# Attention and two feed-forward layers on one core: the value products of a pair's first 256 queries in one visit of TensorE

## The chip, the cores and the metric

One core of a Trainium2 chip runs the whole program in one launch. The metric is the device time of one execution in microseconds (us); runs of one kernel differ by a few hundredths of a per cent here (1092.77 to 1093.15 us in three runs). Everything is fp32, and TensorE, VectorE (DVE), ScalarE (ACT), GpSimd (POOL) and SyncE (SP, which issues most DMAs) each work through a queue of their own in order.

## What is computed

Cut to what matters:

```python
# q, k, v: (4, 8, 576, 64)
q_rot, k_rot = rotate(q), rotate(k)                     # rotary embedding
scores = q_rot @ k_rot.T / 8
attn = exp(scores - max(scores))
attn = attn / (sum(attn) + 1e-9)
x = (attn @ v) as (2304 tokens, 512)
h = x @ w_in;   x = where(h > 0, h, exp(min(h, 0)) - 1) @ w_out       # first layer
h = x @ w2_in;  out = (h - tanh(h)) @ w2_out                          # second layer
```

The change is in the attention alone, in the line `attn @ v`.

## The kernel before

**Pairs and items.** The 32 heads are worked in 16 pairs (numbered 0 to 15). A pair has nine items: for each of the four blocks `u` of 128 queries one item per head (items 0 to 7), and item 8 holds the last 64 queries of both heads. The loop in the attention part runs over all 144 items; below, step s of a pair is the loop's turn `i = 9p + s`, so that steps 9 to 14 of a pair are also steps 0 to 5 of the next.

**One turn of the loop** emits, in this order:

- the row maximum of item i on DVE (`emit_max`, L241);
- the scores of item i + 1 on TensorE (`emit_s`, L232, into one of two PSUM buffers `s`). Each buffer is free again when the exponential two items earlier has read it;
- the exponential of item i on ACT (`emit_exp`, L255);
- `flush`: the copies out of PSUM that were put off in the turn before. Transposes go to `aT` and `aTr` (L286 on DVE, L288 on ACT), a finished product goes to `xa` (L293, always ACT). The transposes' copies are numbered through the whole run, and those whose number leaves 1 or 3 when divided by 5 go to DVE, the others to ACT;
- the normalisation of item i - 1 (`emit_norm`: L268, L269 on DVE, L272 on POOL);
- parts of the next pairs' rotation (`prep`: L148, L150, L153, L157) and of a weight's conversion (L74 to L92);
- the transposes of item i - 4 on TensorE (`emit_t`: L312, L322, and L316 for item 8), into one of three PSUM buffers `pt`;
- the value products that are due (`emit_pv`, L345).

**The value products.** A pair has three groups of queries: group 0 (items 0 to 3, 256 queries), group 1 (items 4 to 7) and group 2 (item 8). A group needs five chunks c of 128 keys, two matmuls each; on the engine each matmul is two weight loads and two matmul instructions, so that a chunk is 4 loads and a whole group is 20. The outputs are 64 wide (one head's dimension) and the moving side is 256 long. The groups 0 and 1 share the one PSUM buffer `o` in turn. The table `PV_AT` says, for each group and chunk, how many turns after the group's last transposes the chunk is emitted:

```python
PV_AT = ((1, 1, 1, 3, 3), (1, 1, 1, 3, 3), (2, 2, 2, 2, 2))
...
pend.append((i + PV_AT[uu // 2][c], pp, uu // 2, c))
```

The last transposes of group 0 are those of item 3, in step 7. So chunks 0 to 2 stand in step 8 and chunks 3 and 4 in step 10. The copy of item 3's transposes, which every chunk needs, is in the flush of step 8: on ACT it stands behind step 8's exponential, on DVE it stands behind step 8's maximum. By the numbering it is on DVE in pairs 2, 4, 7, 9, 12 and 14, and on ACT in the other ten.

**Step 8 to step 12 on TensorE**, before: scores 9, transposes of item 4, 12 loads of products | scores 10, transposes of item 5 | scores 11, transposes of item 6, 8 loads of products | scores 12, transposes of item 7 | scores 13, transposes of item 8 (whose last, L316, waits for the copy of item 7's transposes in the same step's flush), 12 loads of group 1. "Scores 10" are those of the item whose maximum is in step 10, that is of item 1 of the next pair.

**Keys and queries.** The rotated keys and queries of the next pair come through DMAs on SP's queue: `place` copies the second head's keys last (`k<-hl`, L194, four DMAs of a pair, issued after L157 in step 4). Scores 9 are the first that use the new pair's first head, scores 10 the first that use its second head. `load_v` (L137 to L141) loads a pair's values, and `load_w` (L64) a weight.

Of the kernel before, what the change touches and what calls it, by code (L numbers as in the profile page):

```python
# [23 lines left out]
def attention_elu_tanhshrink(ctx: ExitStack, tc: tile.TileContext, qk, v, w1i, w1o, w2i, w2o, tab, out):  # L24
# [35 lines left out]
    def load_w(key, eng=nc.sync):  # L60
        l, kind, c = key
        t = fm[:, 1024 * (nraw[0] % 2):1024 * (nraw[0] % 2) + 1024]
        nraw[0] += 1
        eng.dma_start(out=t.bitcast(mybir.dt.int64), in_=w_src[l, kind][c])  # L64
        raw_t[key] = t
# [43 lines left out]
    with ExitStack() as actx:  # L109
# [20 lines left out]
        def load_qk(p, x):  # L130
            t = p2.tile([128, 2, S], F32, tag=f"t{x}", name=f"t{x}")
            nc.sync.dma_start(out=t, in_=qk[p, :, 2 * x:2 * x + 2, :])
            t_t[p, x] = t

        def load_v(p):
            t = v_t[p] = vt_t[p % 2]
            nc.sync.dma_start(out=t[:, 0:512], in_=v[p, :, 0:512])  # L137
            for h in range(2):
                sl = slice(64 * h, 64 * h + 64)
                nc.sync.dma_start(out=t[sl, 512 + 64 * h:576 + 64 * h], in_=v[p, sl, 512:576])  # L140
            nc.sync.dma_start(out=t[64:128, 640:704], in_=v[p, 0:64, 512:576])  # L141
# [25 lines left out]
        def rotate_first(x):  # L167
            t = t_t.pop((0, x))
            prod = ps_s.tile([128, 2, 512], F32, tag="s", name="prod")[:, :, 0:288]
            for i in range(2):  # L170
                yield
                nc.vector.scalar_tensor_tensor(
                    out=two(t[:, 1, :]) if i else prod, in0=two(t[:, i, :]), scalar=(1.0 if x else SCALE),
                    in1=two(tabs[:, i, :]), op0=ALU.mult, op1=ALU.mult,
                )
            yield
            if x:
                nc.vector.tensor_tensor(out=two(rk), in0=prod, in1=two(t[:, 1, :]), op=ALU.add)
            else:
                for h in range(2):  # L180
                    sl = slice(64 * h, 64 * h + 64)
                    nc.vector.tensor_tensor(
                        out=two(rq[:, h, :])[sl], in0=prod[sl], in1=two(t[:, 1, :])[sl], op=ALU.add
                    )
            yield
# [53 lines left out]
        def emit_max(i):  # L239
            nm = sm.tile([128, 1], F32, tag="nm", name="nm")  # L240
            nc.vector.tensor_reduce(out=nm, in_=s_t[i][:, :, 0:288], axis=AX.XY, op=ALU.max, negate=True)  # L241
            nm_t[i] = nm

        def emit_exp(i):
            p, u, h = items[i]
            s = s_t.pop(i)
            if h in (0, None):
                if u < 4:
                    a_t[p, u] = p3.tile([128, 2, S], F32, tag="a", name="a")
                else:  # L250
                    a_t[p, u] = p1.tile([128, 1, S], F32, tag="a2", name="a2")
                n_t[p, u] = sm.tile([128, 2], F32, tag="den", name="den")
            a = a_t[p, u][:, h or 0, :]
            den = n_t[p, u][:, (h or 0):(h or 0) + 1]
            nc.scalar.activation(  # L255
                out=a.rearrange("p (x c) -> p x c", x=2), in_=s[:, :, 0:288], func=AF.Exp,
                bias=nm_t.pop(i), scale=1.0, accum_out=den,
            )

        def emit_norm(i):  # L260
            p, u, h = items[i]
            if h == 0:
                return
            nh = 2 if h == 1 else 1
            den = n_t.pop((p, u))[:, 0:nh]
            r = sm.tile([128, 2], F32, tag="r", name="r")
            for x in range(nh):
                nc.vector.tensor_scalar_add(den[:, x:x + 1], den[:, x:x + 1], 1e-9)  # L268
            nc.vector.reciprocal(out=r[:, 0:nh], in_=den)  # L269
            for x in range(nh):  # L270
                a = a_t[p, u][:, x, :]
                nc.gpsimd.tensor_scalar(  # L272
                    out=a, in0=a, scalar1=r[:, x:x + 1], scalar2=1.0, op0=ALU.mult, op1=ALU.mult
                )
# [7 lines left out]
        def flush():  # L282
            for out_, in_ in late:
                ev[0] += 1
                if ev[0] % 5 in (1, 3):
                    nc.vector.tensor_copy(out_, in_)  # L286
                else:
                    nc.scalar.copy(out_, in_)  # L288
            late.clear()
            for p, grp, o, n in late_x:  # L290
                b, hp = divmod(p, 4)
                x0 = NTOK * hp + b * S + 256 * grp
                nc.scalar.copy(out=xa[:, x0:x0 + n], in_=o[:, 0:n])  # L293
            late_x.clear()
# [75 lines left out]
        with tc.manual_schedule():  # L370
            for x in range(2):
                t_t[0, x] = p2.tile([128, 2, S], F32, tag=f"t{x}", name=f"t{x}")
            for i in range(2):
                nc.sync.dma_start(out=t_t[0, 1][:, i, :], in_=qk[0, :, 2 + i, :])
                nc.sync.dma_start(out=tabs[:, i, :], in_=tab[:, i, :])
                nc.sync.dma_start(out=t_t[0, 0][:, i, :], in_=qk[0, :, i, :])
            load_qk(1, 1)
            load_qk(1, 0)
            nc.vector.memset(xa[:, 0:512], 0.0)
            nc.vector.memset(zero, 0.0)  # L380
            nc.gpsimd.memset(rq[64:128, 0, :], 0.0)
            nc.gpsimd.memset(rq[0:64, 1, :], 0.0)
            make_identity(nc, ident)
            warm = ps_t.tile([128, 512], F32, tag="pt", name="warm")
            for i in range(8):
                nc.tensor.matmul(out=warm, lhsT=xa[:, 0:128], rhs=xa[:, 0:512], start=True, stop=True)
            for i in range(2):
                nc.scalar.copy(out=qa_t[i][:, S:640], in_=zero)
                nc.scalar.copy(out=qb_t[i][:, 0:64], in_=zero)
                nc.gpsimd.memset(vt_t[i][64:128, 512:576], 0.0)  # L390
                nc.gpsimd.memset(vt_t[i][0:64, 576:704], 0.0)
            rot = [rotate_first(1), rotate_first(0)]
            for i in range(4):
                for r in rot:
                    next(r)
            n = len(items)
            pend = []
            nw = list(range(len(first_w)))[::-1]
            emit_s(0)
            load_v(0)  # L400
            PV_AT = ((1, 1, 1, 3, 3), (1, 1, 1, 3, 3), (2, 2, 2, 2, 2))
            for i in range(n + D + 1):
                p, r = divmod(i, NI)
                for f, *arg in sched.get(i, ()):
                    if f is not prep:
                        f(*arg)
                if i == 7 or i % (2 * NI) == 12:
                    load_w(first_w[nw.pop()]) if nw else None
                if i < n:
                    emit_max(i)  # L410
                if i + 1 < n:
                    emit_s(i + 1)
                if i < n:
                    emit_exp(i)
                flush()
                if 0 <= i - 1 < n:
                    emit_norm(i - 1)
                if p < NPAIR:
                    for f, *arg in sched.get(i, ()):
                        if f is prep:  # L420
                            f(*arg)
                    c = r if p == 1 else NI * (p % 2) + r - 3 if p else -1
                    if c >= 0 and c % 2 == 0 and c // 2 < NCV and p // 2 < len(first_w):
                        key = first_w[p // 2]
                        conv_w(key, c // 2, 512 * (p // 2 % 3))
                if 0 <= i - D < n:
                    emit_t(i - D)
                    pp, uu, hh = items[i - D]
                    if uu in (1, 3) and hh == 1 or uu == 4:
                        for c in range(5):  # L430
                            pend.append((i + PV_AT[uu // 2][c], pp, uu // 2, c))
                for x in [x for x in pend if x[0] <= i]:
                    emit_pv(*x[1:])
                    pend.remove(x)
                if n - 8 <= i < n and (i - n) % 2 == 0:
                    split_x(0, (i - n + 8) // 2)
            while pend:
                emit_pv(*pend.pop(0)[1:])
            flush()
# [521 lines left out]
```

## Time and profile before

| | before |
|---|---|
| median of 3 runs | 1093.11 us (1092.77 to 1093.15) |
| the profiled execution: its own time / its span | 1093.27 us / 1090.8 us |
| TensorE matmul (PE) busy | 1066.9 us, 98% of the span, 6480 instructions |
| TensorE weight loads (PEld) busy | 959.0 us, 88% |
| VectorE busy | 753.3 us, 69% |
| ScalarE busy | 723.1 us, 66% |
| GpSimd busy | 696.5 us, 64% |
| granted TensorE clock | 1.00 of full speed |
| stretch with value products (L345) | 27.4 to 302.7 us |

Matmuls are pipelined and their ends are modelled, so a busy PE need not be PE at its peak. In the attention the weight loads (PEld) show better when TensorE moves on: every matmul has a load of its own, and a load that starts late tells of a wait. The first number of a timeline's row is the start in us from the start of the span, the second how long it lasted; what stands in brackets is idle time of the engine before it, and what ended it.

### The profile page before, as it was taken

The page shows a single profiled execution, that of the slowest core. Times are in us where ns is not written, and L with a number is a line of the kernel's source. Part 1 is how long each engine was busy: PE and PEld are TensorE (multiplying, and loading weights), DVE is VectorE, ACT ScalarE, POOL GpSimd, SP SyncE. Part 2 cuts the span into 40 slices and gives each one's busy share as a digit, 9 for nine tenths or more (in the row PEclk, how much of TensorE's full clock was granted, in tenths as well). Part 3 has the DMA queues.
Part 4 walks back from the last instruction along what each step waited for, and adds up shares of the span by engine and source line. Part 5 has one row for each costly group of instructions (what it writes and reads, how often), then busy time and mean ns, then how long its engine had stood idle before and what let it go on. Part 6 is the DMA issues. An engine that isn't in the chain of part 4 may idle for free.

```text
span 1090.8 us, 18762 instructions
## 1 busy us (share of the span) xinstructions
PE 1066.9 (98%) x6480; PEld 959.0 (88%) x6480; DVE 753.3 (69%) x1436; ACT 723.1 (66%) x1560; POOL 696.5 (64%) x653
## 2 busy tenths in 40 slices
PE   8999999999999999999999999999999999999998
PEld 4777777777799999999999999988998999889986
DVE  7898888888546456675675665376766667766674
ACT  3677677777668656555555555588777877878762
POOL 5887888887568755555555556566567555755552
PEclk9999999999999999999999999999999999999999
DMA  7878777776224344354344672265545664556531
GB/s 237 224 185 214 178 206 195 206 199 173 59 69 143 129 153 136 117 164 166 115 145 139 216 260 81 94 224 202 175 163 176 248 212 175 176 167 221 172 126 58
DMA packets 86590, 182.75 MB, mean 168 GB/s; under 512 B 11745, under 2 KB 47585, under 8 KB 86497
## 3 DMA queue, kind: packets, MB, share of 16 engines
q1 hardware_dynamic: 78720, 153.25, 44.7%
q10 hardware_dynamic: 7776, 28.32, 8.7%
q8 instruction: 51, 0.84, 0.3%
q14 instruction: 43, 0.34, 0.1%
HBM read 127.21 MB, written 27.79 MB: 142 GB/s over the span
## 4 chain that ended last, share of the span: by engine, by line
PE 76%; DVE 11%; POOL 4%; ACT 3%; DMA 3%; issue 2%; SPq 0%; ACTq 0%; DVEq 0%; POOLq 0%
PE y L529 18%; PE h L472 18%; PE yb L723 14%; PE hb L758 9%; PE o L345 6%; PE s L232 5%; PE cvb L758 3%; PE pt L312 3%; DVE nm L241 3%; DVE aT L286 1%; DVE fn L791 1%; DMA qb<-hl 1%; ACT a L255 1%; POOL blk L513 1%; DVE t L150 1%
## 5 line engine op out<-in xcount | busy, mean ns | idle before, releaser
L513 POOL TENSOR_TENSOR gt<-fn,gt 128x384 fp32r<-128x384 f32 x119 | 123.1, 1035 | 78.2 <-ACT gt L512 66.2
L272 POOL TENSOR_SCALAR a<-a,r 128x576 f32<-128x576 f32 x144 | 138.4, 973 | 48.2 <-DVE r L269 31.1
L255 ACT ACTIVATE a<-s,nm 128x576 f32<-128x576 f32 x144 | 107.0, 743 | 90.7 <-DVE nm L241 76.0
L723 PE MATMUL yb<-wb,blk 128*128 128x512 f32 x603 | 154.3, 392 | 0.4 <-POOL blk L513 0.4
L758 PE MATMUL hb<-blk,wa 128*128 128x384 f32 x720 | 139.9, 337 | 2.0 <-DVE fn L791 2.0
L758 PEld LDWEIGHTS hb<-blk,wa 128*128 128x128 f32 x720 | 127.1, 188 | 7.3 <-DVE fn L791 3.0
L723 PEld LDWEIGHTS yb<-wb,blk 128*128 128x128 f32 x603 | 112.5, 188 | 22.6 <-POOL blk L513 0.8
L480 ACT ACTIVATE fn<-h 128x384 f32<-128x384 f32 x96 | 47.3, 493 | 128.4 <-PE h L472 109.6
L241 DVE TENSOR_REDUCE nm<-s 128x1 f32<-128x576 f32 x144 | 107.9, 752 | 28.3 <-PE s L232 25.1
L513 POOL TENSOR_TENSOR blk<-fn,blk 128x384 fp32r<-128x384 f32 x67 | 71.1, 1061 | 87.9 <-ACT blk L512 59.6
L472 PE MATMUL h<-blk,wa 128*128 128x384 f32 x576 | 107.8, 335 | 0.8 <-POOL blk L55 0.6
L529 PE MATMUL y<-gt,wa 128*128 128x384 f32 x576 | 107.7, 334 | 0.1
L529 PE MATMUL y<-gt,wb 128*128 128x384 f32 x576 | 107.5, 334 | 0.0
L472 PE MATMUL h<-blk,wb 128*128 128x384 f32 x576 | 107.5, 334 | 0.0
L497 DVE TENSOR_SCALAR cvb<-fm 128x512 f32<-128x512 f32 x56 | 38.9, 694 | 98.1 <-ACT fm L495 95.7
L472 PEld LDWEIGHTS h<-blk,wa 128*128 128x128 f32 x576 | 100.3, 188 | 1.8 <-POOL blk L55 0.9
L529 PEld LDWEIGHTS y<-gt,wa 128*128 128x128 f32 x576 | 100.5, 188 | 0.4 <-issue 0.4
L529 PEld LDWEIGHTS y<-gt,wb 128*128 128x128 f32 x576 | 100.5, 188 | 0.0
L472 PEld LDWEIGHTS h<-blk,wb 128*128 128x128 f32 x576 | 100.5, 188 | 0.0
L92 POOL TENSOR_TENSOR fm<-fm,fn 128x512 fp32r<-128x512 f32 (+1 forms) x48 | 58.3, 1218 | 55.8 <-ACT fn L91 52.5
L345 PE MATMUL o<-aT,v 128*64 128x256 f32 (+1 forms) x768 | 89.5, 336 | 3.2 <-ACT aT L288 2.8
L148 POOL TENSOR_TENSOR t<-t,tabs 128x576 f32<-128x576 f32 x58 | 82.9, 1430 | 7.2 <-DMA t<-in_qk 7.2
(136 smaller groups left out, 2290.3 us busy)
## 6 DMA issues: line engine op xcount, KB each, us to landing
wa<-wi SPq DMA_DIRECT2D x96, 448.0 KB, 4.9
wb<-wo SPq DMA_DIRECT2D x48, 512.0 KB, 6.4
t<-in_qk SPq DMA_DIRECT2D x30, 576.0 KB, 5.1
k<-hl SPq DMA_DIRECT2D x60, 288.0 KB, 4.4
fm<-in_w2o ACTq DMA_DIRECT2D x16, 512.0 KB, 3.6
fm<-in_w2i ACTq DMA_DIRECT2D x14, 512.0 KB, 3.7
fm<-in_w1i ACTq DMA_DIRECT2D x12, 512.0 KB, 3.7
wi<-fn SPq DMA_DIRECT2D x24, 256.0 KB, 2.2
```

Of the source, the lines that this page charges most:

```text
L92: nc.gpsimd.tensor_tensor(out=lo, in0=f, in1=hi.bitcast(F32), op=ALU.subtract)
L148: eng.tensor_tensor(out=t[:, i, :], in0=t[:, i, :], in1=tabs[:, i, :], op=ALU.mult)
L232: nc.tensor.matmul(out=s[:, half, o0:o0 + n], lhsT=w, rhs=k[:, part, c0:c0 + n], start=(m == 0 and part == 0), stop=(m == len(terms) - 1 a ...
L241: nc.vector.tensor_reduce(out=nm, in_=s_t[i][:, :, 0:288], axis=AX.XY, op=ALU.max, negate=True)
L255: nc.scalar.activation(out=a.rearrange("p (x c) -> p x c", x=2), in_=s[:, :, 0:288], func=AF.Exp, bias=nm_t.pop(i), scale=1.0, accum_out=den,)
L272: nc.gpsimd.tensor_scalar(out=a, in0=a, scalar1=r[:, x:x + 1], scalar2=1.0, op0=ALU.mult, op1=ALU.mult)
L345: nc.tensor.matmul(out=o[sl, 0:n], lhsT=w, rhs=m, start=(c == 0), stop=(c == 4))
L472: nc.tensor.matmul(out=hp, lhsT=w[:, wp, ws], rhs=x_hl(t, xp, c), start=(m == 0), stop=(m == 3 * KC - 1))
L513: nc.gpsimd.tensor_tensor(out=g[:, 1, :], in0=f, in1=g[:, 0, :].bitcast(F32), op=ALU.subtract)
L529: nc.tensor.matmul(out=y_t[e][:, 0:NB], lhsT=w[:, wp, es], rhs=gt[:, gp, :], start=st, stop=sp)
L723: nc.tensor.matmul(out=y, lhsT=gt[:, gp, es], rhs=w[:, wp, :], start=(j == 0 and k == 0), stop=(j == NJ - 1 and k == 2))
L758: nc.tensor.matmul(out=bank, lhsT=w[:, wp, o:o + 128], rhs=x[:, xp, cc, :], start=(start and k == 0), stop=(stop and k == 5), skip_group_c ...
```

## The change

One row of the table: all five chunks of group 0 two turns behind its last transposes, that is in step 9, rather than three chunks in step 8 and two in step 10. Groups 1 and 2 stay.

```diff
-            PV_AT = ((1, 1, 1, 3, 3), (1, 1, 1, 3, 3), (2, 2, 2, 2, 2))
+            PV_AT = ((2, 2, 2, 2, 2), (1, 1, 1, 3, 3), (2, 2, 2, 2, 2))
```

On TensorE's queue, at steps 8 to 10 of pair 0 (`s` scores, `pt` and `pr` transposes, `o` value products of two heads, each row of `o` with x6 standing for 12 loads):

```order
 L232 MATMUL s<-k_193,qa_93 128x288 x4
 L312 MATMUL pt<-ident,a 128x128 x4
-L345 MATMUL o<-aT,v_96 64x256 x6
 L232 MATMUL s<-k_196,qb_95 128x288 x4
 L312 MATMUL pt<-ident,a 128x128 x4
 L322 MATMUL pr<-ident,a 128x128
+L345 MATMUL o<-aT,v_96 64x256 x8
+L345 MATMUL o<-aTr,v_96 64x256 x2
 L232 MATMUL s<-k_193,qa_93 128x288 x4
 L312 MATMUL pt<-ident,a 128x128 x4
-L345 MATMUL o<-aT,v_96 64x256 x2
-L345 MATMUL o<-aTr,v_96 64x256 x2
```

Scores 10 (the fourth row) now stand directly behind step 8's transposes, and all twenty loads of the group stand between step 9's transposes and scores 11 (the row behind them). Scores 12, after the last row, have no products directly before them any more.

On ACT's queue the copy of the finished group 0 (`xa`, the L293 row with 256 columns) is flushed one turn earlier. At the same place of the program (`a` exponentials, `aT` and `aTr` copies of transposes):

```order
 L255 ACTIVATE a,den<-s,nm 128x576
 L288 COPY aTr<-pr 128x128
-L255 ACTIVATE a,den<-s,nm 128x576
-L288 COPY aT<-pt 128x4x128
-L293 COPY xa<-o 128x256
+L293 COPY xa<-o 128x256
+L255 ACTIVATE a,den<-s,nm 128x576
+L288 COPY aT<-pt 128x4x128
 L255 ACTIVATE a,den<-s,nm 128x576
 L288 COPY aTr<-pr 128x128
```

The copy now stands between the exponentials of steps 10 and 11. On SP's queue one load of a weight of the second layer stands earlier, ahead of the last-but-one pair's key copies (`fm` is the buffer of raw weights):

```order
 L64 DMA fm<-in_w1o 128x512
+L64 DMA fm<-in_w2i 128x512
 L194 DMA k_3570<-hl_3532 64x1152 x2
 L194 DMA k_3573<-hl_3532 64x1152 x2
```

The instructions of DVE and POOL stand in the order that they had.

## Rows read from the trace of the kernel before

**Rows 1.** Waits of PEld from 16 to 303 us: total us, times, longest.

```profile
PEld s L232 <- issue: 11.2, 29, 0.4
PEld o L345 <- ACT aT L288: 9.9, 15, 1.5
```

**Rows 2.** Timeline of PEld, pair 8: start us, us, what, and idle before it.

```profile
173.00 1.05 PEld L345 LDWEIGHTS o<-aT,v 128*64 128x64 f32 x10 [0.77 <-ACT aT L288]
174.44 0.56 PEld L232 LDWEIGHTS s<-k,qb 128*128 128x128 f32 x4 [0.38 <-issue]
...
175.40 0.14 PEld L322 LDWEIGHTS pr<-ident,a 128*128 128x128 f32 x1
...
176.02 0.49 PEld L312 LDWEIGHTS pt<-ident,a 128*128 128x128 f32 x4
...
177.69 0.56 PEld L232 LDWEIGHTS s<-k,qb 128*128 128x128 f32 x4 [0.39 <-ACT aT L288]
```

**Rows 3.** Timeline of ACT, pair 8, step 8.

```profile
171.64 0.74 ACT L255 ACTIVATE a<-s,nm 128x576 f32<-128x576 f32 x1 [0.40 <-DVE nm L241]
...
172.37 0.57 ACT L288 COPY aT<-pt 128x512 f32<-128x512 f32 x1
```

**Rows 4.** Timeline of DVE, pair 8, steps 11 and 12.

```profile
176.35 0.76 DVE L241 TENSOR_REDUCE nm<-s 128x1 f32<-128x576 f32 x1
...
178.53 0.76 DVE L241 TENSOR_REDUCE nm<-s 128x1 f32<-128x576 f32 x1 [0.43 <-PE s L232]
```

**Rows 5.** Timeline of PEld, pair 7.

```profile
153.99 0.49 PEld L312 LDWEIGHTS pt<-ident,a 128*128 128x128 f32 x4
154.64 1.06 PEld L345 LDWEIGHTS o<-aT,v 128*64 128x64 f32 x12 [0.17 <-issue]
156.09 0.56 PEld L232 LDWEIGHTS s<-k,qb 128*128 128x128 f32 x4 [0.39 <-issue]
...
162.61 0.14 PEld L316 LDWEIGHTS pr<-ident,a 128*128 128x128 f32 x1 [1.04 <-ACT aT L288]
```

**Rows 6.** Timeline of ACT, pair 7, step 8.

```profile
154.16 0.74 ACT L255 ACTIVATE a<-s,nm 128x576 f32<-128x576 f32 x1
```

**Rows 7.** Timeline of DVE, pair 7, steps 8, 11 and 12.

```profile
153.86 0.68 DVE L286 COPY aT<-pt 128x512 f32<-128x512 f32 x1
...
158.21 0.75 DVE L241 TENSOR_REDUCE nm<-s 128x1 f32<-128x576 f32 x1
...
160.46 0.75 DVE L241 TENSOR_REDUCE nm<-s 128x1 f32<-128x576 f32 x1
```

**Rows 8.** Line L194: fourth key copy in pairs 2, 8, 14; issue, time to landing.

```profile
L194 SPq DMA_DIRECT2D k<-hl x1: 1433/1433/1433, 59.2 to 59.2; - x1
...
DMA to landing us min/median/max: 6.5/6.5/6.5
...
L194 SPq DMA_DIRECT2D k<-hl x1: 1442/1442/1442, 166.6 to 166.6; - x1
...
DMA to landing us min/median/max: 7.0/7.0/7.0
...
L194 SPq DMA_DIRECT2D k<-hl x1: 1145/1145/1145, 271.7 to 271.7; - x1
...
DMA to landing us min/median/max: 6.2/6.2/6.2
```

**Rows 9.** Timeline of DVE, pair 2 step 11, pair 14 steps 11 and 12.

```profile
68.70 0.74 DVE L241 TENSOR_REDUCE nm<-s 128x1 f32<-128x576 f32 x1
...
280.31 0.76 DVE L241 TENSOR_REDUCE nm<-s 128x1 f32<-128x576 f32 x1 [0.29 <-PE s L232]
...
282.49 0.76 DVE L241 TENSOR_REDUCE nm<-s 128x1 f32<-128x576 f32 x1 [0.50 <-PE s L232]
```

**Rows 10.** Timeline of SP's queue, 246 to 254 us.

```profile
246.61 0.55 SPq L64 DMA_DIRECT2D fm<-in_w1o  x1
252.94 1.11 SPq L194 DMA_DIRECT2D k<-hl  x2
```

## The prediction

> **What bounds the kernel now.** The page's busy shares come first: the matmul row is 98% busy, but its ends are modelled, so the waits of the weight loads decide. In the attention stretch two of them belong to the value products [rows 1]: 11.2 us in 29 idle gaps of up to 0.4 us ahead of scores, which nothing that the profile shows ended, and 9.9 us in 15 gaps ahead of products, ended by an ACT copy of transposes. The gaps ahead of scores stand behind product visits, and the second kind is what the change can remove. Next come the timelines, one pair of each sort.
>
> Pair 8 has the copy of item 3's transposes on ACT. Step 8's exponential ends at 171.64 + 0.74 = 172.38, the copy behind it at 172.37 + 0.57 = 172.94 [rows 3], and TensorE's product visit, two loads in, resumes at 173.00 [rows 2]: a stall of 0.77 us. Scores 10 follow at 174.44.
>
> Pair 7 has that copy on DVE. It ends at 153.86 + 0.68 = 154.54 [rows 7], 0.4 us before step 8's exponential does, 154.16 + 0.74 = 154.90 [rows 6]. The visit starts at 154.64, runs its 12 loads without a stall, and scores 10 stand at 156.09 [rows 5].
>
> What ends a pair's middle part is in step 12. The last transposes (L316) need the copy of item 7's transposes, which stands behind step 12's maximum: in pair 7 they wait 1.04 us for it, until 162.61 [rows 5]. Step 12's maximum in turn follows step 11's at once on DVE, or waits for scores 12. So the chain of interest is: scores 11, maximum 11, DVE's work of step 11, maximum 12, copy, L316. TensorE alone does not decide it. Behind L316 the rest of the pair hangs on TensorE's queue, so I let a delay of maximum 12 stay in the end time.
>
> **The change, term by term.** No instruction is added or dropped. Scores 10 lose the 12 loads in front of them, scores 11 get 20 loads in front of them, scores 12 lose 8.
>
> *When can scores 10 start?* Their PSUM buffer is the one that step 8's exponential reads. So they cannot start before that exponential ends, plus the 0.06 us by which loads follow what releases them (172.94 to 173.00 [rows 2, 3]). Before, products filled this time; now TensorE idles. This is the wait that the change adds, and everything behind it on TensorE's queue waits too.
>
> *From scores 10 to maximum 11.* Scores 10 and the transposes of step 9 take 1.10 us (174.44 to 175.40 + 0.14 [rows 2]). A visit of 12 loads takes from the end of the transposes to the next scores 153.99 + 0.49 = 154.48 to 156.09 = 1.61 us [rows 5]; one of 8 loads 176.02 + 0.49 = 176.51 to 177.69 = 1.18 us [rows 2]. That is 0.43 us for four, hence 1.61 + 2 x 0.43 = 2.47 us for 20. From the start of scores to the start of their maximum, where DVE waits for them, are 0.84 us (177.69 to 178.53 [rows 2, 4]). Sum: 4.41 us. So maximum 11 cannot start before the release of scores 10 + 0.06 + 4.41.
>
> *The six pairs with the copy on DVE.* Pair 7: 154.90 + 4.47 = 159.37 against 158.21 [rows 6, 7], 1.16 us later. DVE is busy from there to maximum 12 (158.21 to 160.46, 2.25 us), so the delay reaches it whole. There was no stall to gain from: only the two visits become one, and the larger one stands on the chain.
>
> *The ten with the copy on ACT.* Here the stall pays for most of it. Pair 8 by its exponential: 172.38 + 4.47 = 176.85 against 176.35. DVE's work of step 11 takes 178.53 - 0.43 - 176.35 = 1.75 us [rows 4], which puts maximum 12 at 178.60 against 178.53: before, it waited 0.43 us for scores 12, now it waits for maximum 11, and the two come out alike, 0 to 0.1 us.
>
> *The keys.* Scores 10 are the first that use the second head's new keys, and these were hidden: the fourth copy of pair 8 lands at 166.6 + 7.0 = 173.6 [rows 8], 0.84 us before scores 10 start now, but 1.2 us after the exponential that would release them. With 173.6 as the release, maximum 11 is at 178.07 and maximum 12 at 179.82 against 178.53: 1.29 us. In pair 2 it lands at 59.2 + 6.5 = 65.7, maximum 11 at 70.17 against 68.70 [rows 9]: 1.47 us. In pair 14 it lands at 271.7 + 6.2 = 277.9, maximum 11 at 282.37; DVE's step 11 takes 282.49 - 0.50 - 280.31 = 1.68 us [rows 9], maximum 12 is at 284.05 against 282.49: 1.56 us.
>
> *All pairs by the same working.* The six with the copy on DVE (first pair 2, last pair 14): 1.5, 1.1, 1.2, 1.6, 0.7, 1.6, together 7.7 us. Eight with it on ACT (pairs 1, 3, 5, 6, 8, 10, 11, 13): 0.2, 0.4, 0.2, 0.1, 1.3, 0.1, 0.7, 0.7, together 3.6 us. In pair 0 a long wait for the first DMAs follows, which hides either sign: 0. In pair 15 no scores follow, so one visit fewer gains: 1.61 + 1.18 - 2.47 = 0.32 us. Without the late keys the same sums give 6.0 and 0.5 us.
>
> *Moved on other queues.* ACT's copy of the finished group waits for the 20 loads with step 11's exponential behind it; but that exponential needs maximum 11, which ends over a microsecond after those loads, so nothing is paid. SP's weight load that is moved up costs one issue of 0.55 us in a queue that stands idle from 247.2 to 252.94 [rows 10]: nothing, unless its transfer delays key copies; bound 0 to one issue.
>
> *Sum.* The profiled execution took 1093.27 us with a span of 1090.8; the other 2.5 us lie around the span and stay. 1093.3 + 7.7 + 3.6 - 0.3 = 1104.3 us; the median of the runs is 0.2 us lower, so I say **1104.0 us**. Bounds: the release could cost 0.14 rather than 0.06 us, over 14 pairs + 1.1 us; key copies that land 0.5 us earlier or later relative to the rest take back or add some 3 us.
>
> **Row against rule.** The gaps ahead of scores [rows 1] and 0.17 us ahead of products [rows 5] are paid per visit, and the 0.32 us by which one visit is shorter than two is what they leave. The Trainium skill (TensorEngine Tiling (Array Packing), Key Properties) has a reason for such gaps: a change of the tiling mode, here between 128 x 128 and 128 x 64, drains TensorE; the trace agrees that there is a gap on each side of a visit. By that rule alone the change is a gain, the first rival below.
>
> **Rivals.**
> - *Faster: TensorE is the limit, and the saved visit counts.* Sixteen pairs by 0.32 us give 5.1 us: 1088.2 us. The 98% speak for it, and so does the stall of pair 8. Against it: maximum 12 and L316 are reached through DVE in pair 7, where TensorE waits 1.04 us [rows 5] whatever it did before. It decides if maximum 11 is not what maximum 12 waits for, that is if DVE has more than the 1.2 us of slack that I see none of in pair 7.
> - *The keys stay hidden.* If the key copies land earlier than now, with less traffic at their side, 6.0 + 0.5 - 0.3 remain: 1093.3 + 6.2 - 0.2 = 1099.3 us. For it: usual landings would do, and the late ones are collisions that may move.
> - *Taken back.* The delay of L316 could be slack before the next pair's step 8, where DVE or POOL would have waited anyway: about 1093 us. Against it: TensorE's queue runs from L316 to the next pair's step 8 with hardly a gap.
>
> **Chances.** The forecast with late keys 0.55, hidden keys 0.24, above the range 0.04, taken back 0.07, faster 0.10. A measurement of this kernel can tell about 0.2%, 2.2 us, from no change. So slower has 0.83, same 0.07, faster 0.10. The range 1097.5 to 1106.5 holds the forecast with its bounds and the hidden keys, 0.79 of the chance, and leaves out no change and faster.
>
> **What would show it.** In the changed profile: no stall within a product visit of 20 loads in step 9; scores 10 starting 0.06 us behind step 8's exponential, or behind a key copy's landing, with idle time of TensorE before them; maximum 11 some 4.4 us later; in pairs 2, 4, 7, 9, 12 and 14 L316 later by about a microsecond against the pair's step 8, in the others hardly unless keys are late. The time from the attention's end to the end of the program should stay as it is. I am wrong if scores 11 come no later than before relative to step 8, or if the pairs lengthen without these waits.

## The result and the profile after

The changed kernel takes 1106.49 us (median of four runs, 1105.73 to 1108.06), beside 1093.13 us for the kernel before: a ratio of 1.0124, 95% interval 1.0106 to 1.0141. The prediction said slower, and why; its 1104.0 us was 2.5 us too low, and its range ended at 1106.5.

| | before | after |
|---|---|---|
| the profiled execution: its own time / its span | 1093.27 / 1090.8 us | 1106.37 / 1103.5 us |
| TensorE matmul (PE) busy | 1066.9 us, 98% | 1064.7 us, 96% |
| VectorE / ScalarE / GpSimd busy | 753.3 / 723.1 / 696.5 us | 751.9 / 724.9 / 695.9 us |
| mean granted TensorE clock | 1.000 | 0.998 |
| start of the last value product | 302.7 us | 315.5 us |

No engine has more instructions, and busy times move by 2.2 us at most; what has grown is waits. The waits of TensorE's weight loads in the attention of the changed kernel (total us, times, longest):

```profile
PEld s L232 <- ACT a L255: 22.0, 40, 1.2
PEld s L232 <- issue: 7.3, 18, 0.8
...
PEld pr L316 <- ACT aT L288: 5.0, 3, 1.7
...
PEld o L345 <- ACT aT L288: 3.9, 6, 0.7
```

The stalls in front of products fell from 9.9 us to 3.9, and the gaps ahead of scores that nothing ended from 11.2 to 7.3 [rows 1], the latter in part by name alone: the 0.38 us behind pair 7's visit (below) now stand under an ACT copy. In their place scores wait for exponentials for 22.0 us, against 4.5 us before. DVE's maxima in turn wait more for scores. The page's row for them (busy, mean ns, idle before and what ended most of it), of the kernel before:

```profile
L241 DVE TENSOR_REDUCE nm<-s 128x1 f32<-128x576 f32 x144 | 107.9, 752 | 28.3 <-PE s L232 25.1
```

and of the changed one, with 15.4 us more idle time ended by scores:

```profile
L241 DVE TENSOR_REDUCE nm<-s 128x1 f32<-128x576 f32 x144 | 107.6, 750 | 42.1 <-PE s L232 40.5
```

**Pair 7**, with the copy of item 3's transposes on DVE. Timeline of PEld, changed kernel (answers to [rows 5]):

```profile
158.44 0.56 PEld L232 LDWEIGHTS s<-k,qb 128*128 128x128 f32 x4 [0.91 <-ACT aTr L288]
...
159.72 1.49 PEld L345 LDWEIGHTS o<-aT,v 128*64 128x64 f32 x16 [0.17 <-issue]
161.28 0.36 PEld L345 LDWEIGHTS o<-aTr,v 128*64 128x64 f32 x4
162.03 0.56 PEld L232 LDWEIGHTS s<-k,qa 128*128 128x128 f32 x4 [0.38 <-ACT aTr L288]
...
167.27 0.14 PEld L316 LDWEIGHTS pr<-ident,a 128*128 128x128 f32 x1 [1.68 <-ACT aT L288]
```

ACT's timeline in the same pair, step 8 (answers to [rows 6]):

```profile
157.43 0.74 ACT L255 ACTIVATE a<-s,nm 128x576 f32<-128x576 f32 x1
```

and DVE's, maximum 11 and behind it one row with the maxima 12 and 13 (answers to [rows 7]):

```profile
162.86 0.76 DVE L241 TENSOR_REDUCE nm<-s 128x1 f32<-128x576 f32 x1 [1.96 <-PE s L232]
...
165.13 1.42 DVE L241 TENSOR_REDUCE nm<-s 128x1 f32<-128x576 f32 x2
```

Step 8's exponential ends at 158.17, scores 10 start at 158.44, the 20 loads run without a stall, and from scores 10 to maximum 11 (162.86) are 4.42 us; the prediction had 4.41. Maximum 11 comes 4.69 us behind the exponential's end, against 3.31 before (154.90 to 158.21 [rows 6, 7]). Maximum 12 comes 6.96 us behind it, against 5.56 [rows 7]: the whole 1.4 us arrive there, DVE had no slack. L316 waits 1.68 us instead of 1.04.

**Pair 8**, the copy on ACT. Scores 10 in PEld's timeline of the changed kernel (answers to [rows 2]):

```profile
178.26 0.57 PEld L232 LDWEIGHTS s<-k,qb 128*128 128x128 f32 x4 [1.72 <-ACT aT L288]
```

Step 8's exponential in ACT's timeline (answers to [rows 3]):

```profile
176.31 0.74 ACT L255 ACTIVATE a<-s,nm 128x576 f32<-128x576 f32 x1 [0.43 <-DVE nm L241]
```

Maxima 11 and 12 in DVE's timeline (answers to [rows 4]):

```profile
182.69 0.76 DVE L241 TENSOR_REDUCE nm<-s 128x1 f32<-128x576 f32 x1 [2.35 <-PE s L232]
...
184.36 0.75 DVE L241 TENSOR_REDUCE nm<-s 128x1 f32<-128x576 f32 x1
```

The fourth key copy, by its line: issue and time to landing (answers to [rows 8]):

```profile
L194 SPq DMA_DIRECT2D k<-hl x1: 1443/1443/1443, 171.2 to 171.2; - x1
...
DMA to landing us min/median/max: 6.9/6.9/6.9
```

The exponential ends at 177.05, but the keys land at 171.2 + 6.9 = 178.1: scores 10 start 1.21 us behind the exponential, after 1.72 us of TensorE's idle time. The row puts that down to a copy on ACT, but the copy behind this exponential was done 0.6 us before, and the key is what came last. Maximum 12 is at 184.36 - 177.05 = 7.31 us behind the exponential, against 178.53 - 172.38 = 6.15 [rows 3, 4]: 1.16 us, where 1.29 were worked out.

**What was not predicted** is behind L316 in pair 12. PEld's timeline of the changed kernel there:

```profile
258.62 0.49 PEld L312 LDWEIGHTS pt<-ident,a 128*128 128x128 f32 x4
260.78 0.14 PEld L316 LDWEIGHTS pr<-ident,a 128*128 128x128 f32 x1 [1.67 <-ACT aT L288]
261.04 0.30 PEld L345 LDWEIGHTS o<-aT,v 128*64 128x64 f32 x4
261.53 0.23 PEld L345 LDWEIGHTS o<-aT,v 128*64 128x64 f32 x2 [0.19 <-issue]
...
263.80 0.82 PEld L232 LDWEIGHTS s<-k,qb 128*128 128x128 f32 x4 [0.76 <-issue]
```

and of the kernel before at the same place:

```profile
250.42 0.14 PEld L316 LDWEIGHTS pr<-ident,a 128*128 128x128 f32 x1 [1.57 <-ACT aT L288]
250.68 1.06 PEld L345 LDWEIGHTS o<-aT,v 128*64 128x64 f32 x12
252.13 0.56 PEld L232 LDWEIGHTS s<-k,qb 128*128 128x128 f32 x4 [0.39 <-issue]
```

The 12 loads and the gap behind them take 263.80 - 261.04 = 2.76 us instead of 252.13 - 250.68 = 1.45. The view by windows of the changed kernel says why (start and end of the window, its length, then PE, PEld, DVE, ACT and POOL busy with their instructions, the granted clock, DMA share, GB/s):

```profile
252.00:260.00 8.00, 7.08 (x54) 5.47 (x54) 7.16 (x16) 4.55 (x12) 6.12 (x6) 1.00 0.96 298
260.00:265.00 5.00, 4.22 (x20) 2.57 (x21) 2.79 (x7) 2.36 (x8) 5.00 (x6) 0.66 0.35 115
```

TensorE's clock fell to 1.2 GHz (0.5) from 260.97 to 264.38 us, right behind its wait of 1.67 us for L316. The kernel before waits 1.57 us at that place and keeps 2.4 GHz.

### The profile page after: what moved, and what is told of

Its sections match the earlier page's. It is cut to its first block, busy times and chain, and to the rows that moved or that the text cites. A ratio compares the mean times of both kernels' runs of the same rounds, so it can differ in the third digit from the quotient of the medians.

```text
span 1103.5 us, 18762 instructions
## 1 busy us (share of the span) xinstructions
PE 1064.7 (96%) x6480; PEld 958.9 (87%) x6480; DVE 751.9 (68%) x1436; ACT 724.9 (66%) x1560; POOL 695.9 (63%) x653
## 4 chain that ended last, share of the span: by engine, by line
PE 74%; DVE 11%; POOL 5%; ACT 4%; DMA 3%; issue 3%; SPq 0%; ACTq 0%; POOLq 0%; DVEq 0%
PE y L529 18%; PE h L472 18%; PE yb L723 14%; PE hb L758 9%; PE o L345 6%; PE s L232 4%; DVE nm L241 3%; PE cvb L758 3%; PE pt L312 2%; DVE t L150 1%; DMA v<-in_v 1%; ACT a L255 1%; DMA k<-hl 1%; DVE fn L791 1%; POOL blk L513 1%
## 5 line engine op out<-in xcount | busy, mean ns | idle before, releaser
L272 POOL TENSOR_SCALAR a<-a,r 128x576 f32<-128x576 f32 x144 | 137.9, 969 | 61.5 <-DVE r L269 38.4
L148 POOL TENSOR_TENSOR t<-t,tabs 128x576 f32<-128x576 f32 x58 | 83.8, 1446 | 6.6 <-DMA t<-in_qk 6.6
L312 PE MATMUL pt<-ident,a 128*128 128x128 f32 x576 | 87.0, 274 | 0.1
```

Of the source, the lines that this page charges most:

```text
L148: eng.tensor_tensor(out=t[:, i, :], in0=t[:, i, :], in1=tabs[:, i, :], op=ALU.mult)
L272: nc.gpsimd.tensor_scalar(out=a, in0=a, scalar1=r[:, x:x + 1], scalar2=1.0, op0=ALU.mult, op1=ALU.mult)
L312: nc.tensor.transpose(pt[:, c, :], a[:, h or 0, c0:c0 + 128], ident)
```

## The experiments

**1. The change by pairs.** `dve_pairs` has the new row of the table only in pairs 2, 4, 7, 9, 12 and 14, `act_pairs` only in the other ten.

```diff
-                            pend.append((i + PV_AT[uu // 2][c], pp, uu // 2, c))
+                            at = 2 if uu == 1 and pp in (2, 4, 7, 9, 12, 14) else PV_AT[uu // 2][c]
+                            pend.append((i + at, pp, uu // 2, c))
```

> The change in pairs 2, 4, 7, 9, 12 and 14 alone, those whose copy of item 3's transposes stands on DVE; the other ten as before. Theory (chain through scores 11: scores 10 wait for step 8's exponential, the 20 loads stand ahead of scores 11, maximum 11 and 12 are late): these six pairs carry most of the cost, 8.5 us by the shifts of maximum 12 in the changed kernel, so 1101.6 us, and 1103.2 if TensorE's clock falls again in pair 12. Rival (a cost per moved visit, the same in every pair): 6/16 of 13.4 us, so 1098.1 us.

> The change in the other ten pairs alone, those whose copy of item 3's transposes stands on ACT. Theory (chain): the stall that goes pays for the chain, what is left is late keys in pairs 3, 8 and 11, together 2.9 us, less 0.6 us in pair 15: 1095.4 us, and no fall of the clock, since pair 12 is as before. Rival (the same cost in every pair): 10/16 of 13.4 us, so 1101.5 us.

Beside 1092.92 us for before, `dve_pairs` took 1102.67 us (1.0089, interval 1.0073 to 1.0104) and `act_pairs` 1097.32 us (1.0040, 1.0025 to 1.0055). The first lies between the theory's two values, the second 1.9 us above its value (the section on why the prediction was right or wrong finds them), and both are over 4 us from the rival's: six pairs carry over two thirds, and an equal cost per pair is out. The two add up to the whole (0.0089 + 0.0040 = 0.0129, against 0.0124). The four runs of `dve_pairs` were 1100.45, 1102.33, 1103.02 and 1104.45 us, at mean clocks of 1.000, 0.998, 0.998 and 0.997. The profile is of the slowest, and by its windows (columns as above) it has two falls, behind L316's waits in pairs 2 and 12:

```profile
75.00:79.00 4.00, 4.00 (x19) 2.27 (x20) 1.88 (x2) 1.51 (x5) 4.00 (x5) 0.57 0.16 35
...
259.00:263.00 4.00, 4.00 (x19) 2.47 (x20) 1.82 (x2) 1.45 (x4) 4.00 (x5) 0.57 0.41 134
```

The run at full clock is 7.5 us over before, where the prediction's term for these six pairs was 7.7.

**2. Which part of the visit costs?** `first_visit_late` moves chunks 0 to 2 alone, `second_visit_early` chunks 3 and 4 alone, each to step 9.

```diff
-            PV_AT = ((1, 1, 1, 3, 3), (1, 1, 1, 3, 3), (2, 2, 2, 2, 2))
+            PV_AT = ((2, 2, 2, 3, 3), (1, 1, 1, 3, 3), (2, 2, 2, 2, 2))
```
```diff
-            PV_AT = ((1, 1, 1, 3, 3), (1, 1, 1, 3, 3), (2, 2, 2, 2, 2))
+            PV_AT = ((1, 1, 1, 2, 2), (1, 1, 1, 3, 3), (2, 2, 2, 2, 2))
```

> Chunks 0 to 2 of group 0 in step 9, chunks 3 and 4 in step 10 as before: scores 10 have no products ahead, as in the change, but scores 11 have 12 loads ahead and not 20. Theory (chain): maximum 11 comes 2 x 0.43 = 0.86 us earlier than in the change, so the six pairs with the copy on DVE lose 0.4 us or so each instead of 1.4 (2 to 3.5 us), the others gain up to 0.2 us each but for late keys (+1.4 us in pairs 3, 8, 11): +2 to +4 us, 1095 to 1097 us. Rival (TensorE's idle time ahead of scores 10 is the cost, whatever stands behind): as the change without the fall of the clock, 1105 us.

> Chunks 0 to 2 of group 0 in step 8 as before, chunks 3 and 4 in step 9 instead of step 10: scores 10 start as before, with no new wait for the exponential, but scores 11 get 8 loads ahead of them. Theory (chain): maximum 11 is 1.0 us later in a pair like 7 (156.09 + 1.10 + 1.18 + 0.84 = 159.21 against 158.21) and maximum 12 with it; 0.8 us later in a pair like 8: some 6 + 7 us, 1103 to 1106 us. Rival (the wait of scores 10 is the cost): as before, 1093 us. Late keys play no part here.

Measured: `first_visit_late` 1095.52 us (1.0024, 1.0013 to 1.0035), `second_visit_early` 1106.51 us (1.0128, 1.0111 to 1.0145), half a microsecond above the theory's range and far from the rival's 1093. So TensorE's new wait ahead of scores 10 is cheap by itself: with it and only 12 loads ahead of scores 11 the loss is a fifth. Without that wait, and with 8 loads ahead of scores 11, the whole loss is there, though no key is waited for and in its profile the clock does not fall inside the attention, which ends 12.5 us later than before. What counts is how late scores 11 come. PEld's timeline of `first_visit_late`, scores 10 of pair 7:

```profile
155.06 0.56 PEld L232 LDWEIGHTS s<-k,qb 128*128 128x128 f32 x4 [0.57 <-ACT a L255]
```

and maximum 11 in its DVE timeline:

```profile
158.62 0.76 DVE L241 TENSOR_REDUCE nm<-s 128x1 f32<-128x576 f32 x1 [0.77 <-PE s L232]
```

The same scores 10 of `second_visit_early`:

```profile
161.17 0.56 PEld L232 LDWEIGHTS s<-k,qb 128*128 128x128 f32 x4 [0.38 <-issue]
```

and its maximum 11:

```profile
164.30 0.76 DVE L241 TENSOR_REDUCE nm<-s 128x1 f32<-128x576 f32 x1 [0.94 <-PE s L232]
```

3.56 us for 12 loads and 3.13 us for 8, where the prediction's terms give 1.10 + 1.61 + 0.84 = 3.55 and 1.10 + 1.18 + 0.84 = 3.12.

**3. The copies on DVE in every pair.** `before_dve3` takes the choice of engine from the item rather than from a count: DVE copies the transposes of items 1, 3, 5, 7 and the small one of item 8. `after_dve3` has the same with the changed table.

```diff
-        def evac(out_, in_):
-            late.append((out_, in_))
+        def evac(out_, in_, dve):
+            late.append((out_, in_, dve))
...
-                if ev[0] % 5 in (1, 3):
+                if dve:
...
-            evac(aT[:, h, :, q0:q0 + 128], pt)
+            evac(aT[:, h, :, q0:q0 + 128], pt, i % 9 in (1, 3, 5, 7))
```

> The order of the kernel before, but the copies of the transposes of items 1, 3, 5 and 7 (and the small one of item 8) on DVE in every pair, the other nine of fourteen on ACT, instead of the count by five. Theory (chain): the stall of 0.77 us in a visit goes in the ten pairs that had item 3's copy on ACT, and L316 no longer waits for step 12's exponential and the copy behind it on ACT; 0.3 to 0.6 us of each pair, 1084 to 1089 us. Rival (TensorE's own work is the limit): the stalls become waits elsewhere, 1093 us. Against both: DVE has up to 0.7 us more to do between maxima, in which case it is slower.

> The changed order with the copies of items 1, 3, 5 and 7 on DVE in every pair, to be read against the same placement with the order of before (1087.7 us). Theory (chain): there is no stall to gain from in any pair now, so the change costs in 15 pairs what it costs in a pair like 7, 1.0 to 1.3 us, and 0.3 us is gained in pair 15: +15 to +19 us, 1103 to 1107 us. Rival (the loss hangs on the count by five): +13.4 us or less over 1087.7, 1101 us at most.

`before_dve3` took 1087.67 us (0.9951, 0.9937 to 0.9966): faster than both kernels. `after_dve3` took 1099.91 us, 1.0062 of before (1.0047 to 1.0077), so the change costs 12.2 us on this placement, less than my theory said and inside what I gave the rival, so the time does not decide between them. The traces tell that it is the theory's mechanism at a smaller price. Pair 8 in PEld's timeline of `before_dve3`, the first visit and L316 (here line 315):

```profile
169.17 1.06 PEld L344 LDWEIGHTS o<-aT,v 128*64 128x64 f32 x12 [0.17 <-issue]
...
176.40 0.14 PEld L315 LDWEIGHTS pr<-ident,a 128*128 128x128 f32 x1 [0.21 <-DVE aT L285]
```

Maxima 11 and 12 in its DVE timeline:

```profile
173.35 0.74 DVE L241 TENSOR_REDUCE nm<-s 128x1 f32<-128x576 f32 x1
...
175.01 0.75 DVE L241 TENSOR_REDUCE nm<-s 128x1 f32<-128x576 f32 x1
```

The same two maxima of `after_dve3`:

```profile
178.79 0.76 DVE L241 TENSOR_REDUCE nm<-s 128x1 f32<-128x576 f32 x1 [0.77 <-PE s L232]
...
180.46 0.75 DVE L241 TENSOR_REDUCE nm<-s 128x1 f32<-128x576 f32 x1
```

In the first the visit runs its 12 loads without the stall of [rows 2], and L316 waits 0.21 us. From maximum 11 to 12 DVE takes 1.66 and 1.67 us here, with no idle time that it could give. By the starts of all maxima, maximum 12 comes 5.3 to 5.4 us behind step 8's exponential in pairs 2 to 13 of `before_dve3`, and 6.2 in the same pairs of `after_dve3`: 0.9 us in each, with maximum 11 at 4.6 us in all of the latter, so with keys in time. I had taken the 1.0 to 1.3 us of pairs like 7, whose maximum 11 stood earlier.

**4. The keys.** A first try moved the rotation's last three steps for the keys up by one turn, in the changed kernel and in the one before.

```diff
-                when = [i0 + o for o in ((-10, -6, -4, -3, -2, -1), (-7, -2, 0, 2, 3, 4))[x]]
+                when = [i0 + o for o in ((-10, -6, -4, -3, -2, -1), (-7, -2, 0, 1, 2, 3))[x]]
```

> The changed kernel with the last three steps of the rotation that makes the second head's keys one turn earlier, so that their copies land about 2 us earlier against scores 10. To be read against the kernel before with the same edit. Theory (late keys are 3 to 5 us of the loss): the difference between the two is 13.4 - 4 = 8.5 to 10.4 us. Rival (keys play no part): 13.4 us. Where the steps land between maxima and copies on DVE, both kernels can move alike.

> The kernel before with the same earlier rotation steps: its scores 10 stand behind the first product visit, so keys were never what they waited for. Theory and rival alike: 1093 us, give or take 2 us for DVE work that now stands at another place.

`after_keys_early` took 1107.32 us (1.0132, 1.0117 to 1.0147), `before_keys_early` 1110.94 us (1.0162, 1.0146 to 1.0179). The edit costs the kernel before 18 us by itself, with DVE's work at other places and three falls of the clock in its trace, so the pair tells nothing of keys. Why it costs so much was not followed. The second try takes the transfer away:

```diff
+            if x == 1 and h == 1 and p > 2:
+                k_t[p, 1] = k_t[p - 2, 1]
+                return
```

> The changed kernel, but from pair 3 on the second head's keys aren't copied: the scores use those of pair 1 or 2 that still stand in the two buffers (so x is another from there on; the work of every engine but the DMA queue is the same). Scores 10 then never wait for a key copy. Theory (late keys are part of the loss): scores 10 start 0.14 us behind step 8's exponential in every pair, 3 us less than the changed kernel by the lateness in its trace (pairs 3, 7, 8, 11, 14), 4.8 us less by the prediction: 1101.7 to 1103.5 us. Rival (the keys' traffic is hidden): 1106.5 us.

> The kernel before with the same second head's keys kept, the yardstick of the run above (x is another from pair 3 on here too). Its scores 10 come 0.5 us and more behind the last key copy in nearly all pairs, so 1092 to 1093 us by both; if it gets faster by as much as the changed kernel, what helps there is the missing traffic and not the wait.

`after_keys_kept` took 1102.63 us (1.0083, 1.0066 to 1.0100), `before_keys_kept` 1092.64 us (0.9994, 0.9984 to 1.0003). From 1.0124 the changed kernel gains 0.0041, or 4.5 us, and the kernel before 0.6 us (by its interval between 1.7 and none): late keys are some 4 us of the loss, and the two intervals together leave 2 to 7. In the trace of `after_keys_kept` scores 10 start 0.14 or 0.15 us behind the exponential in every pair, as expected. That trace is of its slowest run, 1105.48 us, which has two falls of the clock, in pairs 8 and 12. The prediction set 4.8 us between its late and its hidden keys; a trace without falls, below, gives 3.1.

**5. The clock.** Fillers in front of L316 keep TensorE at work in its wait; they write to the free buffer `o`. First 12 of them in pairs 2, 7 and 12, then 6 in pair 12.

```diff
                 evac(aT, pt.rearrange("p c (h q) -> p h c q", h=2))
+                if p in (2, 7, 12):
+                    o_t[p, 1] = ps_v.tile([128, 512], F32, tag="o", name="o")
+                    for _ in range(12):
+                        nc.tensor.matmul(out=o_t[p, 1][:, 0:128], lhsT=ident, rhs=ident, start=True, stop=True)
...
-            if c == 0 and grp < 2:
+            if c == 0 and grp < 2 and (p, grp) not in o_t:
```

> The changed kernel with 12 small matmuls (identity by identity, into the free buffer o, overwritten later) in front of L316 in pairs 2, 7 and 12, where TensorE waits 1.67 us for it; estimated at 1.5 us in all, so that they fit in the wait. Nothing is left out. Theory (the fall of TensorE's clock in pair 12 follows that wait and is worth 1.6 to 1.9 us): no stretch at 1.2 GHz inside the attention, some 1104.8 us. Rival (the fall has another cause): it stays, 1106.5 us. If the fillers are longer than the wait, up to 0.5 us more in each of the three pairs.

> Half the fillers, and in pair 12 alone: 6 small matmuls in front of its L316, 1.34 us by the rate at which 12 took 2.68 us, so they fit in the wait of 1.67 us. Theory (the fall of the clock in pair 12 follows TensorE's wait there, worth 1.6 to 1.9 us): no stretch at 1.2 GHz in pair 12 and 1104.7 us where none appears elsewhere. Rival (the fall has nothing to do with the wait): it stays, 1106.5 us.

`after_filler` took 1111.61 us (1.0170, 1.0150 to 1.0189): 12 fillers last 2.68 us and not 1.5, a microsecond longer than the wait, in each of three pairs. `after_filler6` took 1108.37 us (1.0133, 1.0116 to 1.0150). In both the fall in pair 12 is gone, and others came. In `after_filler6` it is at the end of pair 13, where scores 10 waited for a key copy. PEld's timeline there, with loads in twos behind the wait:

```profile
274.22 0.56 PEld L232 LDWEIGHTS s<-k,qb 128*128 128x128 f32 x4 [2.10 <-issue]
...
276.26 0.24 PEld L349 LDWEIGHTS o<-aT,v 128*64 128x64 f32 x2 [0.18 <-issue]
```

and the window that holds them:

```profile
275.00:280.00 5.00, 5.00 (x30) 2.98 (x29) 0.95 (x2) 1.67 (x4) 1.34 (x1) 0.66 0.38 89
```

So neither the theory's time nor the rival's came out, and one fall was traded for another wait and its fall. `after_kept_filler6` therefore joins the kept keys and 6 fillers in pairs 2, 7 and 12; `after_again` is the changed kernel once more.

> The changed order with the second head's keys kept from pair 3 on (x is another from there on) and 6 small matmuls in front of L316 in pairs 2, 7 and 12. No scores wait for keys and TensorE's three longest waits for L316 are filled. Theory (each fall follows a wait of TensorE of over a microsecond, and costs 1.6 to 2 us): no fall in pairs 2, 7 and 12, some 1102.2 us, which is the fastest run with kept keys; with one fall left behind another wait 1104 us. Rival (falls come whatever TensorE waits for): as with kept keys alone, one or two falls, 1102.6 us in the median and up to 1105.5.

> The changed kernel without an edit. Theory (the 2 us by which the prediction was too low are one fall of TensorE's clock): runs lie near 1104.7 us without a fall, 1106.4 with one and 1108 with two, so their spread is far larger than that of the kernel before (0.4 us in one set of runs). Rival (the chain itself is 2 us longer than summed): all runs at 1106.5 within half a microsecond, whatever falls.

`after_kept_filler6` took 1101.09 us (1.0072, 1.0060 to 1.0085), all five runs within 1100.62 to 1101.91, a microsecond under the theory's value, and its profiled run has no fall inside the attention. From maximum 12 of pair 12 to the next step 8's exponential it takes as long as the kernel before, where the changed kernel took 1.6 us more. The window around L316 of pair 12, at 2.4 GHz:

```profile
254.00:262.00 8.00, 7.64 (x61) 6.35 (x59) 7.32 (x16) 4.80 (x12) 6.43 (x7) 1.00 0.50 192
```

and PE's timeline in it (L316 is line 323 here, and 6 fillers are 12 instructions on the engine):

```profile
256.53 1.50 PE L321 MATMUL o<-ident 128*128 128x128 f32 x12
258.14 0.33 PE L323 MATMUL pr<-ident,a 128*128 128x128 f32 x1
```

`after_again` took 1106.29 us (1.0122, 1.0106 to 1.0137), in runs of 1105.03, 1105.41, 1107.17 and 1107.39 us at mean clocks of 1.000, 0.998, 0.997 and 0.997. That they lie apart by 2 us speaks for the theory, but runs of the kernel before in the same set went from 1091.8 to 1094.9, so the spread alone doesn't settle it, and the run of 1105.41 has the fall in pair 12 again, and is 1 us shorter than I expected of such a run. What is shown is the fall's price where it stands: 1.3 us in the visit behind L316, and more in the scores behind it.

## Why the prediction was right or wrong

By the starts of maxima and exponentials in both profiles, the attention's end moved by 12.8 us:

| term | predicted | measured |
|---|---|---|
| exponential 8 to maximum 12, six pairs with the copy on DVE | 7.7 | 7.5 (0.9, 1.2, 1.4, 1.7, 0.8, 1.5) |
| the same, eight pairs with it on ACT | 3.6 | 2.9 (0.1, 0.4, 0.2, 0.1, 1.2, 0.1, 0.8, 0.1) |
| pair 0, and the start before it | 0 | -0.1 (0.4 and -0.5) |
| pair 15 | -0.3 | -0.6 |
| maximum 12 to the next exponential 8, pair 12 | 0 | 1.6 |
| the same, all other pairs | 0 | 1.6 |

The rest of the program follows unchanged (span 12.7 us longer), and 0.4 us more lies around the span of this profiled run.

*Right.* The 4.41 us from scores 10 to maximum 11, the lack of slack on DVE, the split between the six pairs and the others, and the late keys as the ACT pairs' cost. In the pairs whose keys were in time maximum 11 stands 4.57 us behind the exponential's end, where I had 4.47: loads followed their release by 0.14 us, the upper bound that I gave, not by 0.06. Of the keys, pairs 2 and 13 had theirs in time and pairs 8, 11 and 14 late; which pair is hit was only roughly foreseeable, and the sum was. What I set to nothing on ACT's and SP's queues shows nothing: behind the earlier copy of the finished group, step 11's exponential in pair 7 still waits 1.17 us for its maximum, and the keys behind the moved weight load, those of pair 13, were in time.

*The step that failed* is "Behind L316 the rest of the pair hangs on TensorE's queue, so I let a delay of maximum 12 stay in the end time". I carried the delay on and priced nothing behind it: 3.2 us were added there, half of it by the clock of TensorE, of which the prediction says nothing, since the kernel before runs at 1.00 throughout, and for which its range had no room.

The other half is 0.3 to 0.5 us each behind maximum 12 of pairs 1, 6, 8, 10 and 11, all with the copy on ACT (1.8 us, of which others give 0.2 back), and it comes by POOL. In these pairs DVE's idle time ahead of maximum 12 took up 0.3 to 0.5 us of the delay of maximum 11, as predicted for pair 8. But the reciprocal of step 11 (L269) stands ahead of that idle time and carries the whole delay. POOL's normalisation (L272) waits for it, and POOL's products of the rotation (L148) stand behind that. So they come later against maximum 12, and DVE meets them. Pair 1 in the DVE and POOL timelines of the kernel before:

```profile
53.27 0.76 DVE L241 TENSOR_REDUCE nm<-s 128x1 f32<-128x576 f32 x1 [0.37 <-PE s L232]
...
58.37 1.07 DVE L76 TENSOR_SCALAR fm<-fm 128x512 f32<-128x512 f32 x1
...
59.81 0.75 DVE L241 TENSOR_REDUCE nm<-s 128x1 f32<-128x576 f32 x1
...
52.35 1.90 POOL L272 TENSOR_SCALAR a<-a,r 128x576 f32<-128x576 f32 x2 [0.23 <-DVE r L269]
...
57.73 1.42 POOL L148 TENSOR_TENSOR t<-t,tabs 128x576 f32<-128x576 f32 x1
```

and of the changed kernel:

```profile
53.24 0.75 DVE L241 TENSOR_REDUCE nm<-s 128x1 f32<-128x576 f32 x1
...
58.33 1.37 DVE L76 TENSOR_SCALAR fm<-fm 128x512 f32<-128x512 f32 x1
...
60.08 0.75 DVE L241 TENSOR_REDUCE nm<-s 128x1 f32<-128x576 f32 x1
...
52.82 1.83 POOL L272 TENSOR_SCALAR a<-a,r 128x576 f32<-128x576 f32 x2 [0.82 <-DVE r L269]
...
58.01 1.42 POOL L148 TENSOR_TENSOR t<-t,tabs 128x576 f32<-128x576 f32 x1
```

Maximum 12 (53.27 and 53.24) and the start of a weight's conversion (L76) hardly move. L148 moves by 0.28 us, L76 ends some 0.3 us behind its end in both kernels, and the maximum behind L76 is late by as much. Pair 11 repeats this (L76 takes 1.06 and 1.38 us). In pair 10 the rotation's L157 on DVE ends 0.62 us behind L148 in both kernels, and in pairs 6 and 8 its L150, which reads the results of L148, starts 0.03 to 0.04 us behind L148's end in both. The five pairs together give 1.7 to 1.9 us in the profiles of `act_pairs`, `second_visit_early` and `after_kept_filler6` too, where TensorE's clock does not fall inside the attention, and less than 0.1 us in that of `dve_pairs`. This is about what `act_pairs` took over its theory.

*The rivals.* The saved visit counts nowhere but in pair 15: a visit of 20 loads takes 2.48 us in pair 7 (159.41 + 0.14 to 162.03), as summed, yet the loss is there. Hidden keys held in part. In the trace of `after_kept_filler6` the first two rows of the table are 6.6 and 0.7 us, where the prediction without late keys had 6.0 and 0.5; so late keys are 3.1 us of the changed kernel's 10.4 there. Without them, and with the longest waits for L316 filled, 8.5 us of the loss remain (1101.09 against 1092.64), where that rival had 6.2: POOL's part is most of the difference. The delay of L316 was not taken back.

## What to carry to other kernels

Work that is in order behind a shared queue is best put where it delays the consumer that has slack: here the products did least harm in a gap that looked like a stall, and most ahead of the scores that the next maximum waits for. When a new wait is added, price the lateness of everything that was hidden behind the removed one, follow the delay along every engine that it releases and not only along the one that ends the chain (POOL here), and let the range hold what longer waits can set off further on, the clock among it. The stall itself was worth removing, but by moving copies: with those of items 1, 3, 5 and 7 on DVE the kernel is 0.5% faster without moving a product (what each of these copies is worth was not measured).

## What the runs showed of the hardware

A wait of TensorE of 1.7 to 2.1 us inside a busy stretch can be followed by 3.4 us at 1.2 GHz. It stood behind 1.67 us for L316 in the changed kernel, behind 1.68 and 1.67 us in pairs 2 and 12 of `dve_pairs`, and behind 2.10 us ahead of scores 10 in `after_filler6`. A wait doesn't always bring it: 1.68 us in pair 7 of the changed kernel, three waits of 1.67 and 1.68 us in `second_visit_early` and 1.57 us in pair 12 of the kernel before left the clock at 2.4 GHz, and what makes the difference the runs do not tell. In pair 12 of the changed kernel it turned 1.45 us of products into 2.76 us.

DVE's conversions of a weight (L76, L77) take 0.42 to 0.43 us when POOL is idle. In the profiles of the two kernels 13 of them start while POOL's L148 runs: 12 end 0.28 or 0.29 us behind the end of L148, having taken up to 1.68 us. The last one, which started 0.01 us behind L148, took 0.41 us, and L148 1.69 us instead of 1.42.
